# Where half of a causal mask is applied: matmuls on TensorE or selects on GpSimd, in a fused attention and gated-conv kernel

## The chip, the cores and the metric

The kernel runs on one core of a Trainium2 chip. The metric is the device time of one launch in microseconds (us); lower is better. The core has five engines that work side by side, each through its own instructions in order: TensorE (PE, matmuls and transposes; its weight loads are listed as PEld), VectorE (DVE), ScalarE (ACT), GpSimd (POOL) and SyncE (SP, which here only issues DMAs). PE writes its results to PSUM, DVE and ACT read PSUM, and POOL works on SBUF alone.

## The reference

For 8 batches with 8 heads each, 576 positions and 64 numbers per head, an attention with a decay and a causal mask is computed, and behind it a feed-forward layer with a convolution of width 3 along the positions as its gate:

```python
scores = scale * np.matmul(q, k.transpose(0, 1, 3, 2))
log_f = np.log(np.clip(f, 0.0001, 1.0))
cum = np.cumsum(log_f, axis=-1)
decay = cum[:, :, :, None] - cum[:, :, None, :]
causal = np.triu(np.ones((S, S), dtype=bool), k=1)
scores = np.where(causal, -1000000000.0, scores + decay)
attn = np.exp(scores - max)                      # then divided by its row sum
x = (attn @ v)                                   # heads side by side: 576 x 512 per batch
h = np.maximum(x @ w_in, 0.0)                    # 512 -> 1024
conv_out[s] = w0 * h[s - 1] + w1 * h[s] + w2 * h[s + 1]   # per channel
out = (h * sigmoid(conv_out)) @ w_out            # 1024 -> 512
```

All inputs and the output are float32.

## The kernel before

**Tiles and stages.** The unit of the attention is a half batch (hb, 0 to 15): four heads of one batch. Its scores are computed transposed (keys on the 128 partitions, queries along the free axis), in blocks of 128 keys; only blocks on and below the diagonal exist. A pair of heads (i = 2 hb or 2 hb + 1) has its four diagonal blocks per head in one PSUM tile of 128x1024 (`diag_scores`, L344, task sd) and the blocks below the diagonal in one such tile per head (`off_scores`, L366, so). The last 64 keys of all four heads make a tile of 128x256 (`tail_scores`, L324, st). ACT takes the exponential of each (ed L353, eo L371, et L332) into SBUF, `pv` (L384) multiplies with v and a column of ones, in two parts (pv.0, pv.1), DVE divides by the row sum (`norm`, L399, tasks n and m), and the result is transposed by PE (`turn`, t) and copied out by DVE or ACT (tx), or transposed by DMA (tx of hb 11 to 15).

Per batch the feed-forward layer runs over 8 blocks of 128 channels: `ffn1` (L427, task f) on PE, ReLU on ACT (r, L442), the convolution in two instructions on DVE (c L448, d L450), the gate's tanh or sigmoid on ACT (a, L453), the product on DVE (g, L460 or L458), and `ffn2` (L471, task o) on PE over chunks of 128 positions, whose result is evicted from PSUM by ACT or DVE (e, L481; the last batch in parts, L492) and stored by a DMA (s).

**The mask.** On the diagonal blocks half of the scores has to go. There are two ways in the code, chosen per half batch by `MASK_PE` (L88). In it are hb 0 to 7 before the change: PE first writes -1e30 onto the masked places with a matmul of an identity and a constant `mask` (`masked`, L321), one of 128x512 per head of a pair and one of 128x256 for the tail, and the scores are added to that; the exponential goes straight into the f16 tile that pv reads. For the other half batches the scores are not masked; the exponential goes into an f32 tile (`pd`, two buffers, or `p3`, two buffers), and POOL copies it into the f16 tile with an affine_select that writes 0 where the key comes after the query (`diag_mask` L357, task md; `tail_mask` L336, task mt). pv waits for md and mt there, in place of ed and et.

**The decay and the constants.** The decay enters the scores as extra rows of q and k: row images are written to DRAM (ki, L279: three DMAs; zc, L283: four DMAs from tiles that hold 1, -1 and 0) and read back into the q and k tiles (rw, L200: two DMAs, for hb 1 to 7; fi, L193, from hb 8 on). The 1 and -1 (`plus`, `minus`, L253) lie in the second buffer of pd. Half batch 0 adds its decay by matmuls (L317, L319) and doesn't wait for the image. The chain in front of it is dca (DVE, L534), dcl (ACT, L268), dcs (a scan on DVE, L272), dck (DVE, L275 and L276). q and k of hb 0 and 1 are loaded plainly (ld), transposed by PE (tp, L166) and clamped out of PSUM by ACT or DVE (cl, L172, L174); from hb 2 on they come by transposing DMAs (q, L180), clamped in SBUF by DVE (cl, L186) up to hb 7.

**Order.** Nothing is scheduled at run time. Each of these steps is a task with a name, its engine or a choice of engines, its predecessors and the buffers that it takes and gives back (four PSUM tiles, six of pp, two of pd, five of ht, four of u and so on). The string `ORDER` (L17) lists all tasks in one sequence, with the engine behind an @ where there is a choice: the casts of v to f16 (va, L219 and L221) and of the weights (wic, woc, L526) by POOL, ACT or DVE, the copies tx, the evictions e, and the queue that issues ki, rw and the last stores. Each engine executes its tasks in the order of that string, and buffers are handed on in that order too.

Of the kernel before, what the change touches and what calls it, by code (L numbers as in the profile page):

```python
# [56 lines left out]
def kernel(  # L57
# [274 lines left out]
    def tail_exp(hb):  # L332
        o = pt_t[slot[f"et{hb}", "pt"]] if hb in MASK_PE else p3_t[slot[f"et{hb}", "p3"]]
        nc.scalar.activation(o, ps_of(f"st{hb}")[:, 0:HH * SL].rearrange("p (h j) -> p h j", j=SL), AF.Exp, scale=SCALE)
# [18 lines left out]
    def diag_exp(i):  # L353
        o = pair(i)[:, :, 0:512] if i // 2 in MASK_PE else pd_t[slot[f"ed{i}", "pd"]]
        nc.scalar.activation(o, ps_of(f"sd{i}").rearrange("p (s c) -> p s c", s=2), AF.Exp, scale=SCALE)  # L355
# [345 lines left out]
```

## Time and profile before

| | |
|---|---|
| runs of the kernel | 245.07, 245.49, 247.19 us (median 245.49) |
| the profiled execution | its record gives the span from the first to the last instruction, 244.7 us; no time of its own beside it; the median of the runs is 0.8 us above the span |
| granted clock of TensorE | mean 0.993 of full speed |
| instructions | 6393, of which 2627 matmuls |
| DMA | 49.68 MB moved, mean 203 GB/s |

How to read the profile: times are in microseconds from the start of the span, the mean of a group is in nanoseconds. "L322" is line 322 of the kernel. In a group's row stand the line, the engine, the operation, output and inputs by tile name, the shapes and the count; then busy time and mean duration of one; then the idle time of the engine just before these instructions and what ended it. A row of the timeline has start and duration of an instruction (or of several merged ones), and in brackets the idle time in front of it and what released it. A row of busy times by stretch has the stretch, its length, and the busy time of each engine in it with the number of instructions, the granted clock, the share of DMA and its rate. Matmuls are pipelined: a matmul's own duration is longer than the distance to the next one, so PE's pace is read from the distances in the chain of work that ended last. A wait for several semaphores is put down to the one that came last.

### The profile page before, as it was taken

Reading aid. Unit: us, or ns where it says so; the run is one execution under the profiler, and the core shown is the slowest. Engines: PE = TensorE matmul, PEld = TensorE weight load, DVE = VectorE, ACT = ScalarE, POOL = GpSimd, SP = SyncE. Lnnn points to the kernel's source line nnn. Section 1 sums busy time; section 2 is a strip of 40 time slices with the busy share of each in tenths; the row PEclk is TensorE's granted clock in tenths of the full one; section 3 lists DMA queues with packets and bytes.
Section 4 is the critical chain, followed back from the end, with each engine's and each line's share of the span. In section 5 each row is a group of like instructions: output and inputs, shape, how many; then the busy total and the mean of one; then the engine's idle time right before and its main releaser. Section 6 shows DMA issues by size and latency. Waiting matters only on the chain.

```text
span 244.7 us, 6393 instructions
## 1 busy us (share of the span) xinstructions
PE 228.6 (93%) x2627; PEld 146.1 (60%) x2627; DVE 205.5 (84%) x324; ACT 206.8 (85%) x278; POOL 51.9 (21%) x77
## 2 busy tenths in 40 slices
...
GB/s 189 334 169 250 278 184 189 223 198 306 196 216 196 169 182 220 238 268 251 224 212 274 194 198 269 270 102 196 265 198 227 195 209 4 106 173 77 171 85 216
DMA packets 120424, 49.68 MB, mean 203 GB/s; under 512 B 109879, under 2 KB 110647, under 8 KB 120395
## 3 DMA queue, kind: packets, MB, share of 16 engines
...
q10 hardware_dynamic: 322, 0.47, 0.6%
q8 instruction: 20, 0.33, 0.6%
...
HBM read 21.11 MB, written 10.17 MB: 128 GB/s over the span
## 4 chain that ended last, share of the span: by engine, by line
PE 81%; DMA 5%; DVE 5%; ACT 5%; issue 1%; SPq 1%; ACTq 0%; DVEq 0%
PE ps L476 26%; PE ps L431 23%; PE ps L314 15%; PE ps L391 7%; DMA qk<-image 3%; PE ps L322 3%; PE ps L396 3%; DMA u<-in_f_dram 2%; PE ps L416 2%; ACT qk L172 2%; DVE u L450 2%; DVE u L448 1%; ACT ht L442 1%; ACT pp L372 1%; PE ps L317 1%
## 5 line engine op out<-in xcount | busy, mean ns | idle before, releaser
L431 PE MATMUL ps<-xt,w_in_f 128*128 128x512 f16 (+1 forms) x512 | 71.0, 288 | 0.4 <-DVE xt L419 0.4
L372 ACT ACTIVATE pp<-ps 128x1024 f16<-128x1024 f32 x64 | 64.8, 1032 | 3.7 <-PE ps L314 2.3
L476 PE MATMUL ps<-w_out_f,hg 128*128 128x512 f16 x288 | 66.8, 379 | 0.0
L314 PE MATMUL ps<-qk 128*128 128x128 bf16 (+2 forms) x576 | 63.9, 241 | 2.1 <-DMA qk<-image 0.9
L448 DVE SCALAR_TENSOR_TENSOR u<-ht,cwt 128x576 f32<-128x576 f16 x64 | 52.4, 832 | 4.4 <-ACT ht L442 4.2
L450 DVE SCALAR_TENSOR_TENSOR u<-ht,cwt,u 128x576 f32<-128x576 f16 x64 | 53.9, 856 | 0.5
L453 ACT ACTIVATE hg<-u,cw 128x576 f16<-128x576 f32 x64 | 48.7, 782 | 6.1 <-DVE u L450 6.0
L431 PEld LDWEIGHTS <-w_in_f 128*128 128x128 f16 x512 | 34.7, 99 | 29.4 <-issue 1.3
L314 PEld LDWEIGHTS <-qk 128*128 128x128 bf16 x576 | 39.4, 98 | 19.2 <-issue 2.5
L442 ACT ACTIVATE ht<-ps 128x576 f16<-128x576 f32 x64 | 41.0, 664 | 6.4 <-PE ps L431 2.8
L476 PEld LDWEIGHTS <-hg 128*128 128x128 f16 x288 | 26.9, 98 | 28.9
L460 DVE SCALAR_TENSOR_TENSOR hg<-hg,ht 128x576 f16<-128x576 f16 x51 | 38.6, 767 | 0.6 <-ACT hg L453 0.5
L358 POOL TENSOR_SCALAR_AFFINE_SELECT pp<-pd 128x1024 f16<-128x1024 f32 x16 | 19.7, 1244 | 53.6 <-ACT pd L355 53.6
L391 PE MATMUL ps<-va,pp 128*128 128x65 f16 x640 | 25.3, 194 | 1.7 <-DVE va L219 1.7
L391 PEld LDWEIGHTS <-pp 128*128 128x128 f16 x640 | 23.0, 98 | 4.2 <-DVE va L219 1.9
L407 DVE TENSOR_TENSOR xm<-ps,rc 128x896 f16<-128x896 f32 (+1 forms) x32 | 23.9, 751 | 0.5
L355 ACT ACTIVATE pp<-ps 128x1024 f16<-128x1024 f32 x16 | 16.6, 1038 | 5.2 <-PE ps L314 4.0
L219 POOL CAST va<-vf 128x1024 f16<-128x1024 f32 x8 | 10.0, 1247 | 34.3 <-PE ps L314 18.8
L355 ACT ACTIVATE pd<-ps 128x1024 f32<-128x1024 f32 x16 | 16.2, 1023 | 1.2 <-PE ps L314 0.5
L405 DVE RECIPROCAL rc<-ps 128x14 f32<-128x14 f32 (+1 forms) x32 | 6.6, 207 | 10.2 <-PE ps L396 4.9
L322 PE MATMUL ps<-mask,ident 128*128 128x512 bf16 (+1 forms) x40 | 14.4, 364 | 0.4 <-ACT pp L372 0.3
L481 ACT COPY ob<-ps 128x1024 f32<-128x1024 f32 (+1 forms) x14 | 12.9, 918 | 0.3 <-issue 0.2
...
## 6 DMA issues: line engine op xcount, KB each, us to landing
...
```

Of the source, the lines that this page charges most:

```text
L314: nc.tensor.matmul(o, tk[:, h * S + k0:h * S + k0 + 128], tq[:, h * S + q0:h * S + q0 + n], start=first, stop=last and not by_matmul(hb, h))
L355: nc.scalar.activation(o, ps_of(f"sd{i}").rearrange("p (s c) -> p s c", s=2), AF.Exp, scale=SCALE)
L372: nc.scalar.activation(pair(i)[:, s, 512:1536], ps_of(f"so{i}.{s}"), AF.Exp, scale=SCALE)
L391: nc.tensor.matmul(ps[:, c:c + D + 1], block(hb, h, m, n), va[:, h, m, 0:D + 1], start=(m == 0), stop=(m == n))
L407: nc.vector.tensor_tensor(xm[:, CUT * D * u:CUT * D * u + nj * k * D].rearrange("p (j x d) -> p j x d", x=k, d=D), got[:, :, :, 0:D], r.un ...
L431: nc.tensor.matmul(ps[:, t0:t1], w_in_f16[:, cc, 128 * ff:128 * (ff + 1)], xt[:, cc // 2, x:x + t1 - t0], start=(cc == 0), stop=(cc == NCC ...
L442: nc.scalar.activation(ht_of(b, ff)[:, 2:2 + S], ps_of(f"f{b}.{ff}")[:, 0:S], AF.Relu, scale=1.0 if (b, ff) in LATE else 0.5)
L448: nc.vector.scalar_tensor_tensor(u, ht[:, 1:1 + S], cwt[:, ff, 0:1], ht[:, 2:2 + S], op0=ALU.mult, op1=ALU.add)
L450: nc.vector.scalar_tensor_tensor(u, ht[:, 3:3 + S], cwt[:, ff, 1:2], u, op0=ALU.mult, op1=ALU.add)
L453: nc.scalar.activation(hg_of(b, ff), u_t[slot[f"c{b}.{ff}", "u"]], AF.Sigmoid if (b, ff) in LATE else AF.Tanh, scale=cw[:, ff, 1:2])
L460: nc.vector.scalar_tensor_tensor(hv, hv, 1.0, ht_of(b, ff)[:, 2:2 + S], op0=ALU.add, op1=ALU.mult)
L476: nc.tensor.matmul(ps[:, 512 * j:512 * (j + 1)], w, w_out_f16[:, ff, :], start=(ff == 0), stop=(ff == NFF - 1))
```

## The change

`MASK_PE` is cut to half batches 0 to 3. For hb 4 to 7 the mask matmuls go (16 of 128x512 and 4 of 128x256), their exponentials write f32 tiles, and eight tasks md8 to md15 and four tasks mt4 to mt7 are added on POOL. The tile of zeros becomes 128 partitions high, and 1 and -1 are held in its upper half instead of in a buffer of pd. ORDER is replaced as a whole.

```diff
-    MASK_PE = (0, 1, 2, 3, 4, 5, 6, 7,)
+    MASK_PE = (0, 1, 2, 3,)
...
-    zero = cpool.tile([64, 2 * S], BF16, name="zero")
+    zeros = cpool.tile([128, 2 * S], BF16, name="zeros")
+    zero = zeros[0:64]
...
-    signs = pd_t[1].rearrange("p s c -> p (s c)").bitcast(BF16)
-    plus, minus = (signs[0:BH, x * S:(x + 1) * S] for x in range(2))
+    plus, minus = (zeros[BH:128, x * S:(x + 1) * S] for x in range(2))
```

In the new ORDER these tasks have another engine:

| tasks | before | after |
|---|---|---|
| va2.0, va9.0, va15.0, va1.1 | DVE | POOL |
| va3.0, va3.1, va4.0, va5.1, va11.1, va12.1, va14.0, va15.1 | ACT | POOL |
| va8.0, va7.1 | ACT | DVE |
| va8.1; va9.1; va14.1 | DVE; POOL; POOL | ACT; ACT; DVE |
| wic3, woc2 | POOL | DVE |
| e1.1, e2.1, e3.2, e5.1 | ACT | DVE |
| e7.3, e7.1.1; e7.4, e7.1.0 | DVE; ACT | ACT; DVE |
| tx0; tx10 | DVE; ACT | ACT; DVE |
| cl0.0.0, cl1.1.1 | ACT | DVE |
| ki, rw1, rw2; rw5 | SP; ACT | ACT; SP |
| s7.2 | SP | ACT |

Its beginning, up to the first ffn1, in the order of each engine (before, then after):

```
PE   cw tp0.0.0 tp0.0.1 tp0.1.0 tp0.1.1 sd0 so0.1 tp1.0.0 so0.0 tp1.0.1 sd1 tp1.1.0 tp1.1.1 so1.1 so1.0 st0 pv0.0 sd2 so2.1 st1 so2.0 sd3 so3.1 so3.0 pv0.1 sd5 pv1.0 so5.1 t0 pv1.1 sd4 t1 f0.0
PE   tp0.0.0 tp1.0.0 cw tp0.0.1 tp0.1.0 tp0.1.1 tp1.0.1 sd0 tp1.1.0 so0.0 tp1.1.1 so0.1 sd1 so1.0 so1.1 sd2 st1 so2.1 pv0.0 sd3 st0 so3.0 so3.1 sd4 so2.0 pv0.1 sd5 pv1.0 t0 pv1.1 so5.1 t1 so4.1 st2 f0.0
DVE  dca dcs dck cwt cl0.1.1 cl1.0.1 va1.1 cl1.1.0 cl2.0 cl2.1 n0.0 m0.0 n0.1 m0.1 n1.0 m1.0 tx0 n1.1 m1.1 tx1 cl3.0 cl3.1 c0.0
DVE  dca cl0.0.0 dcs cwt dck cl1.0.1 cl0.1.1 cl1.1.0 cl1.1.1 cl2.0 cl2.1 n0.0 m0.0 cl3.0 n0.1 cl3.1 m0.1 n1.0 m1.0 n1.1 m1.1 tx1 wic3 c0.0
ACT  dcl cl0.0.0 cl0.0.1 cl0.1.0 ed0 eo0.1 eo0.0 cl1.0.0 ed1 cl1.1.1 eo1.1 eo1.0 et0 ed2 eo2.1 et1 eo2.0 ed3 eo3.0 eo3.1 ed5 eo5.1 ed4 r0.0
ACT  dcl cl1.0.0 cl0.0.1 cl0.1.0 ki ed0 eo0.0 rw1 eo0.1 ed1 eo1.0 eo1.1 ed2 et1 rw2 eo2.1 ed3 et0 eo3.0 eo3.1 eo2.0 ed4 ed5 tx0 eo5.1 eo4.1 r0.0
SP   ld0.0.0 ld0.1.0 ld0.0.1 v0.0 ld0.1.1 ld1.0.1 ld1.0.0 v0.1 v0.2 v0.3 v0.4 ki q2.1 q2.0 wi1 rw1 wi0 wi2 wi3 rw2 q3.0 q3.1 q4.1 v1.0
SP   ld0.0.0 ld1.0.0 ld0.0.1 ld0.1.1 ld0.1.0 ld1.0.1 v0.0 q2.1 v0.2 v0.1 v0.3 q2.0 v0.4 q3.0 q3.1 wi0 wi1 v1.0 wi3 wi2 rw3 q5.0
```

POOL's list around the new masks, and the end of PE's list:

```
POOL after   va1.0 va0.0 va1.1 va0.1 wic0 wic1 wic2 va2.0 va2.1 va3.0 va3.1 woc0 md9 woc3 woc1 md8 mt4 va4.0 va5.0 va5.1 md11 md10 mt5 md13 md12 va6.0 va6.1 mt6 md14 md15 mt7 md19 md18
PE after     ... sd13 so13.1 pv5.1 sd12 t4 so12.0 t5 so13.0 so12.1 f2.0 f2.1 sd15 so15.0 f2.2 st6 pv6.0 st7 f2.3 ...
PE after     ... o7.4.6 o7.3.5 o7.4.7 o7.1.1 o7.2.4 o7.3.6 o7.2.5 o7.0.5 o7.3.7 o7.1.2 o7.0.6 o7.2.6 o7.1.3 o7.0.7 o7.2.7 o7.1.4 o7.1.5 o7.1.6 o7.1.7
```

More of the change, by code (lines that the diff above doesn't have):

```diff
@@ new lines @@
+ld0 ld1 ld0.0.0 ld1.0.0 tp0.0.0 tp1.0.0 dca cl0.0.0@DVE ld0.0.1 dcl dcs cw ld0.1.1 cwt ld0.1.0 cl1.0.0@ACT dck tp0.0.1
+tp0.1.0 ld1.0.1 tp0.1.1 v0.0 cl0.0.1@ACT tp1.0.1 cl0.1.0@ACT cl1.0.1@DVE ki@ACT q2.1 sd0 cl0.1.1@DVE v0.2 v0.1 tp1.1.0
+ed0 v0.3 q2.0 so0.0 tp1.1.1 cl1.1.0@DVE so0.1 cl1.1.1@DVE va1.0@POOL v0.4 eo0.0 sd1 rw1@ACT q3.0 so1.0 eo0.1 ed1 so1.1
+cl2.0 va0.0@POOL sd2 eo1.0 eo1.1 cl2.1 st1 ed2 et1 so2.1 pv0.0 sd3 rw2@ACT va1.1@POOL q3.1 n0.0 m0.0 st0 va0.1@POOL
+wi0 so3.0 eo2.1 so3.1 ed3 cl3.0 wic0@POOL wi1 et0 wic1@POOL eo3.0 sd4 v1.0 eo3.1 so2.0 pv0.1 wi3 eo2.0 n0.1 cl3.1 sd5
@@ new lines @@
+wi2 pv1.0 m0.1 ed4 n1.0 ed5 m1.0 t0 pv1.1 so5.1 tx0@ACT n1.1 m1.1 rw3@SP eo5.1 q5.0 t1 v1.1 tx1@DVE wic3@DVE so4.1 st2
+eo4.1 v1.3 f0.0 f0.1 r0.0 f0.2 r0.1 so5.0 c0.0 et2 d0.0 r0.2 wic2@POOL v1.4 f0.3 f0.4 c0.1 c0.2 h0 v1.2 a0.0 g0.0 d0.1
+q4.1 eo5.0 r0.3 so4.0 f0.5 r0.4 d0.2 eo4.0 a0.2 sd6 cl5.0 r0.5 c0.4 so6.1 so6.0 c0.5 f0.6 ed6 g0.2 eo6.0 q4.0 sd7
+so7.0 va2.0@POOL d0.5 r0.6 eo6.1 d0.4 va2.1@POOL c0.3 v2.0 a0.1 a0.4 pv2.0 pv2.1 n2.0 m2.0 ed7 st3 n2.1 eo7.0
+va3.0@POOL cl4.1 m2.1 so7.1 cl4.0 d0.3 t2 eo7.1 va3.1@POOL wo0 pv3.0 f0.7 rw4@ACT c0.6 q5.1 wo3 et3 g0.4 v2.4 wo1
@@ new lines @@
+pv3.1 d0.6 n3.0 tx2@ACT n3.1 r0.7 st4 a0.6 m3.0 m3.1 a0.3 sd9 et4 g0.6 ed9 t3 tx3@DVE sd8 c0.7 cl5.1 g0.1 ed8 so9.1
+woc0@POOL g0.3 wo2 eo9.1 rw5@SP md9 d0.7 so8.1 eo8.1 f1.0 r1.0 a0.5 c1.0 f1.1 v2.1 q6.0 a0.7 g0.5 f1.2 r1.2 r1.1 f1.3
+f1.4 so9.0 woc3@POOL f1.5 g0.7 d1.0 r1.3 sd10 woc2@DVE h1 r1.4 v2.2 a1.0 woc1@POOL c1.1 g1.0 d1.1 eo9.0 c1.3 md8 ed10
+a1.1 o0.0 sd11 o0.1 ed11 c1.2 so10.0 c1.4 d1.2 r1.5 so10.1 v2.3 q6.1 d1.3 e0.0@ACT eo10.0 eo10.1 so8.0 f1.6 g1.1 mt4
+eo8.0 r1.6 o0.2 c1.5 d1.4 st5 va4.0@POOL d1.5 pv4.0 so11.1 et5 cl6.0 va5.0@POOL so11.0 va4.1@DVE a1.5 o0.3 cl6.1 g1.5
@@ new lines @@
+a1.4 q7.0 n4.0 eo11.1 va5.1@POOL c1.6 md11 md10 eo11.0 m4.0 pv4.1 f1.7 n4.1 cl7.0 q7.1 a1.3 e0.1@ACT v3.0 r1.7 rw6@SP
+m4.1 pv5.0 sd13 so13.1 cl7.1 n5.0 mt5 v3.2 m5.0 a1.2 q8.1 ed13 pv5.1 n5.1 sd12 t4 m5.1 eo13.1 g1.4 ed12 so12.0 md13 t5
+so13.0 tx4@DVE md12 eo12.0 v3.4 tx5@DVE g1.2 eo13.0 v3.3 so12.1 c1.7 eo12.1 f2.0 r2.0 f2.1 rw7@SP r2.1 g1.3 sd15
+so15.0 v3.1 va6.0@POOL ed15 eo15.0 f2.2 st6 d1.6 c2.0 et6 q9.1 d1.7 d2.0 pv6.0 st7 va6.1@POOL n6.0 c2.1 r2.2 f2.3 et7
+sd14 m6.0 a1.6 a1.7 mt6 ed14 f2.4 zc pv6.1 g1.7 md14 r2.4 h2 d2.1 a2.0 f2.5 n6.1 m6.1 g1.6 so15.1 o1.0 a2.1 r2.3 g2.0
@@ new lines @@
+so14.1 eo15.1 r2.5 q9.0 g2.1 c2.2 q8.0 md15 t6 va7.0@DVE eo14.1 f2.6 d2.2 fi9 q10.0 c2.4 a2.2 r2.6 mt7 tx6@DVE fi8
+c2.6 g2.2 so14.0 o1.1 eo14.0 f2.7 e1.0@ACT r2.7 sd19 pv7.0 st9 v4.0 q11.1 va7.1@DVE sd18 c2.5 v4.3 c2.7 q11.0 ed19
+n7.0 et9 v4.2 d2.4 pv7.1 v4.1 m7.0 ed18 n7.1 o1.2 so19.0 so18.1 md19 s0.0 m7.1 d2.5 a2.4 c2.3 d2.7 q10.1 d2.3 a2.5 t7
+o1.3 eo18.1 g2.5 eo19.0 v4.4 sd17 a2.3 tx7@DVE ed17 e1.1@DVE fi11 f3.0 s1.0 sd16 g2.4 fi10 a2.7 r3.0 g2.3 f3.1 md18
+ed16 r3.1 so18.0 d2.6 c3.1 f3.2 r3.2 eo18.0 a2.6 v5.0 va9.0@POOL so16.1 o1.4 c3.0 so16.0 eo16.1 f3.3 eo16.0 f3.4 d3.0
@@ new lines @@
+g3.7 f4.2 r4.1 f4.3 c4.1 g3.4 eo21.1 r4.2 mt10 r4.0 f4.4 d4.1 c4.0 va10.0@POOL q12.0 s1.2 r4.3 so22.1 d4.0 so23.0
+so21.0 c4.3 md20 h4 r4.4 eo23.0 eo22.1 eo21.0 o3.0 va11.0@POOL st11 c4.4 q13.0 d4.4 d4.3 a4.4 et11 c4.2 so23.1 d4.2
+o3.1 a4.0 pv10.0 va10.1@DVE eo23.1 a4.1 n10.0 pv10.1 e3.0@ACT a4.2 m10.0 g4.1 mt11 n10.1 g4.4 pv11.0 fi12 n11.0 a4.3
+fi13 f4.5 m10.1 r4.5 m11.0 va11.1@POOL f4.6 sd25 g4.0 q15.1 so25.0 r4.6 v6.0 sd24 pv11.1 ed25 n11.1 s3.0 m11.1 ed24
+c4.5 f4.7 eo25.0 md25 r4.7 sd27 d4.5 g4.2 sd26 t10 tx10@DVE ed27 g4.3 o3.2 a4.5 md24 so27.0 md27 o3.3 eo27.0 so24.0
```

24 lines of the change are left out of this document (23 added, 1 removed).

## The prediction, made before the result was known

> **What bounds the kernel now.** I read the page first, then busy time by stretch, then what VectorE (DVE) waits for, then single groups and pieces of the timeline.
>
> ```profile
> span 244.7 us, 6393 instructions
> ...
> PE 228.6 (93%) x2627; PEld 146.1 (60%) x2627; DVE 205.5 (84%) x324; ACT 206.8 (85%) x278; POOL 51.9 (21%) x77
> ...
> PE 81%; DMA 5%; DVE 5%; ACT 5%; issue 1%; SPq 1%; ACTq 0%; DVEq 0%
> ```
>
> TensorE (PE) carries 81% of the chain that ended last. Shares of the whole span hide the stages, so I cut at the first and last conv work of DVE, c0.0 at 39.9 and the end of g7.7 at 236.2. Columns: length, then busy time of PE, weight loads, DVE, ACT, POOL with counts, granted clock, DMA share, GB/s.
>
> ```profile
> 39.90:236.20 196.30, 193.50 (x2196) 119.62 (x2195) 183.19 (x274) 179.72 (x249) 40.04 (x39) 0.99 0.90 197
> ```
> ```profile
> 62.00:110.00 48.00, 47.99 (x583) 30.89 (x583) 46.13 (x70) 46.02 (x65) 4.66 (x5) 1.00 1.04 210
> ```
> ```profile
> 50.40:53.90 3.50, 3.50 (x36) 2.27 (x33) 3.12 (x6) 3.50 (x6) 0.00 (x0) 0.51 1.18 250
> ```
>
> In those 196.3 us PE is idle for 2.8, DVE for 13.1 and ACT for 16.6. PE sets the pace, but two engines stand close behind it: from 62 to 110, where the masks to be removed lie, PE has no idle time and DVE 1.9 us in 48. The third row is a stretch at half the granted clock. In front of it lies the longest idle time of PE behind the start-up:
>
> ```profile
> 49.99 1.62 PE L391 MATMUL ps<-va,pp 128*128 128x65 f16 x32 [1.67 <-DVE va L219]
> ```
> ```profile
> 151.56 1.73 PE ps L476 x8
> ```
>
> pv2.0 waits 1.67 us for va2.0, which stands on DVE behind conv work; then 3.5 us at 0.51 lose another 1.7. The second row is the chain: eight 128x512 matmuls in 1.73, so 0.216 us for 512 columns. That is PE's real pace; the durations of 380 ns in the groups overlap.
>
> **The change part by part.** The groups that price it (mean ns of one after the comma):
>
> ```profile
> L358 POOL TENSOR_SCALAR_AFFINE_SELECT pp<-pd 128x1024 f16<-128x1024 f32 x16 | 19.7, 1244 | 53.6 <-ACT pd L355 53.6
> ...
> L322 PE MATMUL ps<-mask,ident 128*128 128x512 bf16 x32 | 12.4, 386 | 0.4 <-ACT pp L372 0.3
> ...
> L219 POOL CAST va<-vf 128x1024 f16<-128x1024 f32 x8 | 10.0, 1247 | 34.3 <-PE ps L314 18.8 <-DMA vf<-in_v_dram 10.0 <-PE ps L431 5.5
> ...
> L526 POOL CAST w_out_f<-ob 128x1024 f16<-128x1024 f32 x4 | 5.5, 1392 | 13.4 <-DMA ob<-in_moe_w_out_dram 13.4
> ...
> L481 DVE COPY ob<-ps 128x1024 f32<-128x1024 f32 x3 | 3.7, 1219 | 2.0 <-ACT xt L419 1.9
> L219 DVE CAST va<-vf 128x1024 f16<-128x1024 f32 x4 | 3.6, 910 | 0.5 <-DMA out_dram<-ob 0.5
> ...
> L337 POOL TENSOR_SCALAR_AFFINE_SELECT pt<-sel_q 128x256 f16<-128x256 f32 x4 | 2.6, 644 | 23.0 <-ACT sel_q L334 23.0
> ...
> L322 PE MATMUL ps<-mask,ident 128*128 128x256 bf16 x8 | 2.1, 272 | 0.0
> ...
> L492 DVE COPY u<-ps 128x512 f32<-128x512 f32 x2 | 1.4, 692 | 2.1 <-ACT ob L492 1.9 <-PE ps L476 0.2
> ```
>
> *Masks off PE.* Half batches 4 to 7 lose half of the 32 and half of the 8: 16 x 0.216 + 4 x 0.108 = 3.9 us. The exponentials keep their length (their output turns from f16 to f32). POOL gains eight selects at 1.244 and four at 0.644: 12.5 us.
>
> *The stall.* va2.0 moves to POOL, behind casts that end early. So 1.67 + 1.7 = 3.4 us more can go from PE. If something else is late there (sd7 or so7.0 hold their PSUM slots longer), nothing is gained: 0 to 3.4. PE alone could then end at 244.7 - 3.9 - 3.4 = 237.4.
>
> *Work that changes engines.* After c0.0, DVE gains the evictions e1.1, e2.1, e5.1 (3 x 1.22), e3.2 (0.69), the cast woc2 (taken as a cast of va, 0.91), tx10 (0.75, the rows below), and goes from four large casts of va to two (-1.82) and from three small ones to four (below half of a large one; 0.3): 4.5 us. ACT loses those evictions, tx10, four large casts and four small ones net: at DVE's prices 3.7 + 0.7 + 0.8 + 3.6 + 1.2, some 10 us. POOL gets six large casts of va (7.5) and three small ones (1.5), gives woc2 (-1.4): with the masks 20 us on top of 40.
>
> *POOL against DVE.* Where the two meet, the trace shows an instruction of DVE that takes 0.81 or 0.82 by itself doubled:
>
> ```profile
> 39.85 0.81 DVE L448 SCALAR_TENSOR_TENSOR u<-ht,cwt 128x576 f32<-128x576 f16 x1
> ```
> ```profile
> 120.36 0.82 DVE L450 SCALAR_TENSOR_TENSOR u<-ht,cwt,u 128x576 f32<-128x576 f16 x1
> 121.09 0.75 DVE L460 SCALAR_TENSOR_TENSOR hg<-hg,ht 128x576 f16<-128x576 f16 x1
> 121.76 1.65 DVE L450 SCALAR_TENSOR_TENSOR u<-ht,cwt,u 128x576 f32<-128x576 f16 x1
> 123.34 1.58 DVE L219 CAST va<-vf 128x1024 f16<-128x1024 f32 x1
> ```
> ```profile
> 121.39 2.98 POOL L358 TENSOR_SCALAR_AFFINE_SELECT pp<-pd 128x1024 f16<-128x1024 f32 x2 [7.39 <-ACT pd L355]
> ```
> ```profile
> L450 DVE SCALAR_TENSOR_TENSOR u<-ht,cwt,u 128x576 f32<-128x576 f16 x64 | 53.9, 856 | 0.5
> L448 DVE SCALAR_TENSOR_TENSOR u<-ht,cwt 128x576 f32<-128x576 f16 x64 | 52.4, 832 | 4.4 <-ACT ht L442 4.2
> ...
> L460 DVE SCALAR_TENSOR_TENSOR hg<-hg,ht 128x576 f16<-128x576 f16 x51 | 38.6, 767 | 0.6 <-ACT hg L453 0.5
> ```
>
> Two selects in a row cost DVE 0.83 and, against the mean cast of 0.91, 0.67: 1.5 us in 2.98. On average it is far less: the means of the three conv groups lie 41 and 17 ns above 815 and 17 above 750, so 64 x 0.041 + 64 x 0.017 + 51 x 0.017 = 4.6 us, with that slow cast 5.3 us in 40 us of POOL, 0.135 for each. For 20 us more I take 2.7; the ends are 0 (all in DVE's idle time) and 0.5 x 20 = 10.
>
> The Trainium skill speaks against this part: "SBUF — State Buffer", section "Who interferes with whom", has a DVE instruction with two SBUF inputs and a GpSimd instruction that reads SBUF fight for one port, which the first holds to its end while the other stands still. By that rule alone, with DVE always the later, the 20 us would cost DVE nearly 20, with POOL always the later nothing; the average of this trace is near the second, the pair at 121 us near the first.
>
> *New waits.* pv4 to pv7 now wait for POOL instead of ACT. In POOL's queue md12 stands in front of va6.0, and pv6.0 needs both: that is the closest place.
>
> ```profile
> 89.15 1.02 ACT L355 ACTIVATE pp<-ps 128x1024 f16<-128x1024 f32 x1 [0.21 <-PE ps L314]
> ```
> ```profile
> 94.81 0.99 PE ps L391 x32
> ```
>
> That exponential (ed12) ends at 90.2; one select and one cast end at 92.7, at the pace of the slow pair above at 93.2; pv6.0 begins at 94.8. So cover is 1.5 us or more; without it PE idles for the difference, and past some 1.7 the half clock comes back.
>
> *Constants.* plus and minus move into a tile of their own partitions: same memsets, same DMAs. It lets ed8 and ed9 write pd before zc has sent the rows. Nothing.
>
> *Start-up.* On DVE cl0.0.0 goes ahead of the scan, and the weight ratios ahead of dck; q of half batch 1 is loaded second.
>
> ```profile
> 8.37 1.36 DVE L272 TENSOR_TENSOR_SCAN u<-one,u 128x576 f32<-128x576 f32 x1 [0.75 <-ACT u L268]
> ...
> 10.26 0.76 DVE L276 SCALAR_TENSOR_TENSOR kc<-u,kc 64x576 bf16<-64x576 f32 x1
> ...
> 12.22 0.58 PE L322 MATMUL ps<-mask,ident 128*128 128x512 bf16 x1
> ...
> 12.29 1.47 DVE L174 TENSOR_SCALAR qk<-ps,lim 128x1152 uint16<-128x1152 uint16 x1
> ```
>
> The copy of 1.47 fills the 0.75 us in which the scan waited and 0.7 more, and the ratios, which filled the time from dck's end at 11.0 to 12.3, come ahead of it: dck ends at 11.0 + 0.7 + 1.3 = 13.0. sd0, at 12.2 before, starts 0.8 late; PE uses the time for two more transposes of inputs (0.5 each) that came later before. Net 0. ki's three DMA issues and rw1's and rw2's two each move from SP to ACT, past SP's weight and q loads; behind ki only ed0 stands, which waits for sd0; behind rw1 (which waits for the last clamp, cl1.1.1) stands eo0.1, perhaps 1 us. ACT loses two clamps for it; rw5 goes back to SP and s7.2 to ACT, an issue or two each, beside other work. I take 0, bounds -1 and +2. At the end of it tx0 goes to ACT:
>
> ```profile
> 35.75 0.75 DVE L419 COPY xt<-ps 128x1152 f16<-128x1152 f16 x1
> ...
> 37.51 0.76 DVE L419 COPY xt<-ps 128x1152 f16<-128x1152 f16 x1 [0.46 <-PE ps L416]
> ```
>
> The second copy released f0.0; it can come 0.65 sooner, so c0.0 starts at 39.2.
>
> **The sum.** PE alone would end at 237.4, but DVE can't follow: its 183.2 become 183.2 + 4.5 + 2.7 = 190.4 us. What stays of its 13.1 us of idle time is the term that decides. Its waits from 62 to 228 us:
>
> ```profile
> DVE u L448 <- ACT ht L442: 3.3, 8, 0.6
> DVE ob L481 <- ACT xt L419: 1.9, 1, 1.9
> DVE xt L419 <- PE ps L416: 1.4, 4, 0.6
> DVE rc L405 <- PE ps L396: 0.8, 3, 0.4
> DVE rc L405 <- PE ps L391: 0.8, 2, 0.6
> DVE hg L460 <- ACT hg L453: 0.5, 2, 0.3
> ```
>
> 5.7 us were for ACT, which gets 10 us lighter, and 3.0 for PE, which gets 7 lighter. I take both away: 13.1 - 8.7 = 4.4; the ends are 0 and 13.1. Behind the end of g7.7 lay 8.5 us, 21 matmuls of 0.216 in it; the new list has 17 from the first that needs g7.7: 7.6. So 39.2 + 190.4 + 4.4 + 7.6 = 241.6 us of span. The median of the runs shown, 245.49, stands 0.8 above the profiled span: 242.4.
>
> **The rivals.**
>
> *PE keeps setting the pace.* DVE's idle time goes to nearly 0 and the POOL meetings fall into it: 237.4 + 0.8 = 238.2, or 241.7 if the stall is only replaced. For it: the chain is 81% PE, and ACT's relief unties DVE. Against it: it needs DVE busy for 98 to 100% of 190 us, and no stretch above has more than 96%.
>
> *The start-up or a late POOL result takes the gain back.* A stall like that at 48 us in a new place, with half clock, costs 3.4; from 242.4 that gives 245.8, no change. For it: an order that is new throughout; against it: the 1.5 us of cover at pv6.0.
>
> *DVE becomes the bound and POOL holds it (slower).* If each us of added POOL work costs DVE 0.5 instead of 0.135, as at 121 us, that is 10 instead of 2.7: 242.4 + 7.3 = 249.7. It turns into a loss from 2.7 + 3.1 = 5.8 us, 0.29 for each. For it: the masks land where DVE has 4% of air. This is the rule of "SBUF — State Buffer" with DVE the later one half of the time.
>
> **How the numbers follow.** The forecast 242.4 has 0.45 (its own range 240.3 to 244.5), PE keeps the pace 0.25, no change by a new stall 0.13, slower by the port 0.17. The range 238.0 to 248.5 leaves out the lower edge of the second and the worse half of the last. 1% is 2.45 us, about what a measurement here can tell from nothing: faster is below 243.0. That is 0.6 of the forecast and nearly all of PE's case: 0.27 + 0.23 = 0.50; slower 0.17; same 0.33.
>
> **What would show it.** Right: 20 mask matmuls at L322; no wait for va ahead of pv2.0 and no half clock near 50 us; between c0.0 and g7.7 DVE busy for about 190 us with under 6 idle, and PE with several us of idle time, released by DVE or ACT. The terms: means of the three conv groups of DVE (856, 832 and 767 now) up by 10 to 20 ns; the time of c0.0 (39.2). Wrong: DVE idle by over 8 us while PE stands still too (a wait that I don't see), selects that release pv6.0, or a PE that is busy throughout while the span goes below 239.

## The result, and the profile after

The change made the kernel slower: 264.81 us (median; 263.24 to 266.15) against 245.56 us, ratio 1.078 with an interval of 1.0712 to 1.0847. The forecast was 242.4 with a range up to 248.5; the kernel went the other way. Of the variants below, e4, e5 and e10 had executions that took longer than the rest of theirs (up to 599.57 us in e5); their medians and ratios leave these out, and e4's profile is of one of them (257.2 us). In the profile after, the lines of the untouched code stand 52 or 53 further down (L448 is now L500, L358 is L410, L219 is L272). The head of the page:

```profile
span 262.0 us, 6376 instructions
...
PE 229.7 (88%) x2607; PEld 145.8 (56%) x2607; DVE 233.0 (89%) x330; ACT 197.5 (75%) x264; POOL 82.0 (31%) x97
...
DVE 46%; PE 42%; ACT 4%; issue 4%; DMA 2%; ACTq 0%; SPq 0%; DVEq 0%
```

What sets the pace has changed: DVE carries 46% of the chain that ended last, where it carried 5%, and PE 42% instead of 81%. DVE is busy for 27.5 us more than before, though only a few pieces of work were moved onto it. Busy time by stretch, from the first conv instruction (c0.0) to the end of the last gate (g7.7), and for the stretch in which the removed masks lay:

```profile
37.90:252.80 214.90, 193.46 (x2170) 118.61 (x2169) 208.37 (x278) 171.20 (x235) 70.83 (x60) 0.98 0.83 183
...
62.00:115.00 53.00, 46.49 (x574) 29.82 (x573) 52.72 (x70) 43.62 (x60) 21.60 (x19) 0.97 0.88 172
```

DVE is busy for 208.4 of 214.9 us, and for all but 0.3 of the 53 us of the second row. PE, which had 2.8 us of idle time between these two points, now has 21.4. The groups show where DVE's time comes from:

```profile
L500 DVE SCALAR_TENSOR_TENSOR u<-ht,cwt 128x576 f32<-128x576 f16 x64 | 59.7, 948 | 1.6 <-ACT ht L494 1.5
L502 DVE SCALAR_TENSOR_TENSOR u<-ht,cwt,u 128x576 f32<-128x576 f16 x64 | 58.8, 936 | 0.5
...
L410 POOL TENSOR_SCALAR_AFFINE_SELECT pp<-pd 128x1024 f16<-128x1024 f32 x24 | 34.2, 1434 | 59.9 <-ACT pd L407 59.9
...
L512 DVE SCALAR_TENSOR_TENSOR hg<-hg,ht 128x576 f16<-128x576 f16 x51 | 47.3, 945 | 0.6 <-ACT hg L505 0.6
...
L272 POOL CAST va<-vf 128x1024 f16<-128x1024 f32 x14 | 17.8, 1280 | 50.8 <-DMA vf<-in_v_dram 50.8
```

There are as many instructions in the three conv groups as before (64, 64 and 51), and each does the same work; but their means went from 832, 856 and 767 to 948, 936 and 945 ns. By the prediction's own formula, 64 x (mean - 815), again 64 x (mean - 815), and 51 x (mean - 750), that is 8.5 + 7.7 + 9.9 = 26.2 us of lengthening, where the trace of before had 4.6. The selects grew too, from a mean of 1244 to 1434 ns. How that comes about is seen best where one engine runs conv work while the other has several tasks in a row. DVE, then POOL, of the same stretch:

```profile
187.73 0.75 DVE L512 SCALAR_TENSOR_TENSOR hg<-hg,ht 128x576 f16<-128x576 f16 x1
188.39 1.59 DVE L500 SCALAR_TENSOR_TENSOR u<-ht,cwt 128x576 f32<-128x576 f16 x1
189.91 1.64 DVE L502 SCALAR_TENSOR_TENSOR u<-ht,cwt,u 128x576 f32<-128x576 f16 x1
191.47 1.58 DVE L512 SCALAR_TENSOR_TENSOR hg<-hg,ht 128x576 f16<-128x576 f16 x1
192.98 0.81 DVE L502 SCALAR_TENSOR_TENSOR u<-ht,cwt,u 128x576 f32<-128x576 f16 x1
```
```profile
188.28 1.09 POOL L272 CAST va<-vf 128x1024 f16<-128x1024 f32 x1 [9.73 <-DMA vf<-in_v_dram]
189.33 1.61 POOL L410 TENSOR_SCALAR_AFFINE_SELECT pp<-pd 128x1024 f16<-128x1024 f32 x1
190.89 1.55 POOL L272 CAST va<-vf 128x1024 f16<-128x1024 f32 x1
```

POOL runs a cast, a select and a cast back to back; exactly three instructions of DVE take 1.6 us instead of 0.75 to 0.82, and the next one, with POOL idle, takes 0.81 again. From the second POOL task on, both engines are slow: they take turns.

The waits moved with it. PE's longest idle time behind the start-up is no longer at pv2.0 but at 69 us. One row each of PE's and ACT's timeline, and busy time by stretch:

```profile
69.20 1.01 PE L366 MATMUL ps<-qk 128*128 128x64 bf16 x4 [3.06 <-ACT ht L494]
```
```profile
67.83 0.78 ACT L505 ACTIVATE hg<-u,cw 128x576 f16<-128x576 f32 x1 [3.33 <-DVE u L502]
```
```profile
66.00:68.00 2.00, 0.14 (x2) 0.04 (x1) 2.00 (x3) 0.17 (x1) 1.20 (x2) 1.00 1.10 230
68.00:70.00 2.00, 0.80 (x4) 0.45 (x4) 2.00 (x4) 2.00 (x4) 0.00 (x0) 0.60 1.03 232
70.00:72.00 2.00, 2.00 (x13) 0.89 (x10) 2.00 (x4) 2.00 (x4) 0.00 (x0) 0.54 1.53 239
```

Read backwards: PE waits 3.06 us for a PSUM tile that ACT's ReLU (L494) has to empty; ACT was itself idle for 3.33 us, waiting for DVE's `u`; DVE is busy without a gap (2.00 of 2.00 in each row). When PE goes on, its clock is near half of full speed. So the delay is paid twice on PE, as idle time and in a slower clock.

### The profile page after: what moved, and what is told of

Read it like the earlier page. It is cut to its first block, busy times and chain, and to the rows that moved or that the text cites. A ratio compares the mean times of both kernels' runs of the same rounds, so it can differ in the third digit from the quotient of the medians.

```text
span 262.0 us, 6376 instructions
## 1 busy us (share of the span) xinstructions
PE 229.7 (88%) x2607; PEld 145.8 (56%) x2607; DVE 233.0 (89%) x330; ACT 197.5 (75%) x264; POOL 82.0 (31%) x97
## 4 chain that ended last, share of the span: by engine, by line
DVE 46%; PE 42%; ACT 4%; issue 4%; DMA 2%; ACTq 0%; SPq 0%; DVEq 0%
DVE u L500 13%; PE ps L528 13%; DVE hg L512 12%; DVE u L502 10%; PE ps L483 10%; PE ps L366 7%; PE ps L443 4%; DVE qk L239 3%; DVE xm L459 3%; PE ps L219 2%; DMA hg<-in_q_dram 2%; PE ps L448 2%; DVE xt L471 2%; DVE ob L533 2%; ACT hg L505 1%
## 5 line engine op out<-in xcount | busy, mean ns | idle before, releaser
L424 ACT ACTIVATE pp<-ps 128x1024 f16<-128x1024 f32 x64 | 63.5, 1023 | 6.4 <-PE ps L371 3.5
L500 DVE SCALAR_TENSOR_TENSOR u<-ht,cwt 128x576 f32<-128x576 f16 x64 | 59.7, 948 | 1.6 <-ACT ht L494 1.5
L502 DVE SCALAR_TENSOR_TENSOR u<-ht,cwt,u 128x576 f32<-128x576 f16 x64 | 58.8, 936 | 0.5
L410 POOL TENSOR_SCALAR_AFFINE_SELECT pp<-pd 128x1024 f16<-128x1024 f32 x24 | 34.2, 1434 | 59.9 <-ACT pd L407 59.9
L494 ACT ACTIVATE ht<-ps 128x576 f16<-128x576 f32 x64 | 40.6, 653 | 14.1 <-DVE hg L512 5.8
L512 DVE SCALAR_TENSOR_TENSOR hg<-hg,ht 128x576 f16<-128x576 f16 x51 | 47.3, 945 | 0.6 <-ACT hg L505 0.6
L272 POOL CAST va<-vf 128x1024 f16<-128x1024 f32 x14 | 17.8, 1280 | 50.8 <-DMA vf<-in_v_dram 50.8
L407 ACT ACTIVATE pd<-ps 128x1024 f32<-128x1024 f32 x24 | 24.3, 1026 | 2.3 <-PE ps L366 1.9
L239 DVE TENSOR_SCALAR qk<-qk,lim 128x2304 uint16<-128x2304 uint16 x12 | 11.0, 924 | 3.4 <-DMA qk<-in_q_dram 3.4
L219 PE MATMUL ps<-ident_b,hg 128*128 128x128 bf16 x72 | 7.6, 289 | 6.0 <-DMA hg<-in_q_dram 6.0
L219 PEld LDWEIGHTS <-hg 128*128 128x128 bf16 x72 | 6.6, 134 | 6.2 <-DMA hg<-in_q_dram 6.2
```

The source lines that it names most:

```text
L410: nc.gpsimd.affine_select(pair(i)[:, :, 0:512].rearrange("p s (m j) -> p s m j", j=128), pd_t[slot[f"ed{i}", "pd"]].rearrange("p s (m j) - ...
L424: nc.scalar.activation(pair(i)[:, s, 512:1536], ps_of(f"so{i}.{s}"), AF.Exp, scale=SCALE)
L494: nc.scalar.activation(ht_of(b, ff)[:, 2:2 + S], ps_of(f"f{b}.{ff}")[:, 0:S], AF.Relu, scale=1.0 if (b, ff) in LATE else 0.5)
L500: nc.vector.scalar_tensor_tensor(u, ht[:, 1:1 + S], cwt[:, ff, 0:1], ht[:, 2:2 + S], op0=ALU.mult, op1=ALU.add)
L502: nc.vector.scalar_tensor_tensor(u, ht[:, 3:3 + S], cwt[:, ff, 1:2], u, op0=ALU.mult, op1=ALU.add)
L512: nc.vector.scalar_tensor_tensor(hv, hv, 1.0, ht_of(b, ff)[:, 2:2 + S], op0=ALU.add, op1=ALU.mult)
```

## The experiments

My theory: every POOL instruction that reads SBUF and meets a conv instruction of DVE lengthens it by some 0.7 us; the sum of these meetings, on an engine with 3% of idle time, is the loss. The first rival: the new order is bad by itself (stalls, half clock, POOL results that come late), and the longer instructions are a side effect. The second: the added masks alone cost it. Medians, ratios to the kernel before on the same chip (with intervals), and the lengthening by the formula above:

| kernel | us | ratio | lengthening, us |
|---|---|---|---|
| before | 245.56 | 1 | 4.6 |
| after | 264.81 | 1.078 (1.0712 to 1.0847) | 26.2 |
| e1_write_only_masks | 250.53 | 1.0205 (1.0185 to 1.0226) | 10.5 |
| e2_write_only_pool | 243.85 | 0.9935 (0.9913 to 0.9957) | 0.7 |
| e3_new_order_pe_masks | 259.17 | 1.054 (1.0485 to 1.0595) | 18.8 |
| e6_new_order_old_casts | 261.91 | 1.0624 (1.0566 to 1.0683) | 20.6 |
| e7_new_order_alone | 256.13 | 1.0428 (1.0384 to 1.0472) | 15.1 |
| e12_new_order_write_only | 248.05 | 1.0094 (1.0058 to 1.0131) | 0.8 |
| e4_old_order_pool_masks | 252.92 | 1.0318 (1.0273 to 1.0363) | see there |
| e5_old_order_new_casts | 251.1, 248.9 | 1.0167 (1.0097 to 1.0237) | 10.4 |
| e11_one_half_batch | 247.13 | 1.0046 (1.0013 to 1.0079) | 6.9 |
| e10_va2_on_pool | 247.14 | 1.0025 (0.9981 to 1.0069) | 6.1 |
| e9_before_write_only | 246.46 | 1.0018 (0.9985 to 1.005) | 0.6 |

**The same kernel with POOL only writing.** e1 leaves ORDER and every task where it is, but its masks fill their tile without reading, and the exponential writes the f16 tile in place of the f32 one; e2 does the same to POOL's casts of v, which then no longer wait for v to be loaded either.

```diff
 def diag_exp(i):
-    o = pair(i)[:, :, 0:512] if i // 2 in MASK_PE else pd_t[slot[f"ed{i}", "pd"]]
+    o = pair(i)[:, :, 0:512]
 def diag_mask(i):
-    nc.gpsimd.affine_select(pair(i)[:, :, 0:512]..., pd_t[slot[f"ed{i}", "pd"]]..., ...)
+    nc.gpsimd.memset(pair(i)[:, :, 0:512], 0.5)
...
+    if e == "POOL":                                   # e2 only
+        nc.gpsimd.memset(va[:, :, 0:4, 0:D] if part == 0 else va[0:SL, :, 4, 0:D], 0.5)
```

> The changed kernel (264.8 us), but all 36 masks of GpSimd write a constant instead of reading scores: the exponential goes straight into the f16 tile and a memset of the same tile follows it, so that the order, the engine and the wait of pv for GpSimd stay (left out: the mask and the diagonal scores). Theory 'shared reading' (a GpSimd instruction that reads SBUF holds up VectorE instructions with two SBUF inputs): the selects stand beside about 15 us of lengthened VectorE instructions in the changed trace, so about 250 us (247 to 254), and the means of the three conv groups fall from 948, 936, 945 to about 880. Rival 'the order' (the new list makes engines wait whatever GpSimd does): 262 to 266. Rival 'late masks' (pv waits for GpSimd): 262 to 266, since the chain is as long.

> As e1, and the casts of v on GpSimd are memsets too (left out as well: half of v). Shared reading: nearly all lengthening goes, 238 to 244 us, conv means at 820 to 840. The order: 258 or more. Late masks: as e1, 260 or more, since masks still come from GpSimd.

Measured: 250.53 and 243.85 us. The groups of e1, then of e2, and e2's busy time from c0.0 to the end of g7.7:

```profile
L495 DVE SCALAR_TENSOR_TENSOR u<-ht,cwt 128x576 f32<-128x576 f16 x64 | 55.3, 878 | 2.8 <-ACT ht L489 2.6
...
L408 POOL MEMSET pp<- 128x1024 f16 x24 | 22.6, 951 | 59.6 <-ACT pp L405 59.6
```
```profile
L497 DVE SCALAR_TENSOR_TENSOR u<-ht,cwt 128x576 f32<-128x576 f16 x64 | 50.8, 808 | 3.3 <-ACT ht L491 2.9
L499 DVE SCALAR_TENSOR_TENSOR u<-ht,cwt,u 128x576 f32<-128x576 f16 x64 | 51.5, 822 | 0.5
...
L410 POOL MEMSET pp<- 128x1024 f16 x24 | 22.7, 952 | 77.0 <-ACT pp L407 77.0
L509 DVE SCALAR_TENSOR_TENSOR hg<-hg,ht 128x576 f16<-128x576 f16 x51 | 38.1, 764 | 0.5 <-ACT hg L502 0.4
```
```profile
39.56:233.06 193.50, 187.84 (x2170) 116.37 (x2169) 182.87 (x278) 170.58 (x235) 44.39 (x60) 1.00 0.93 202
```

POOL still runs 60 tasks in the stretch, at the same places of every queue and each for about 0.95 us where it was a mask of 128x1024. It lengthens nothing: 808, 822 and 764 ns. DVE's busy time is 182.9 instead of 208.4 us with the same 278 instructions, and the whole loss is gone: 264.81 to 243.85, of which 14.3 us go with the masks' reading and 6.7 with the casts'. This rules out the first rival in its plain form. Stalls and half clock went too (in that stretch PE is idle for 5.7 us instead of 21.4, at a granted clock of 1.00), so in the kernel after they follow from a late DVE.

**The order, the masks and the casts apart.** e3 takes the new ORDER without the twelve added mask tasks, with the masks of hb 4 to 7 back on PE. e6 is the kernel after with the 17 casts of v that changed engine back on their old ones. e7 does both, so that the new order alone is left, with POOL's selects and casts of v those of before.

```diff
-MASK_PE = (0, 1, 2, 3,)                                    # e3, e7; their ORDER lacks md8 to md15 and mt4 to mt7
+MASK_PE = (0, 1, 2, 3, 4, 5, 6, 7,)
-va1.1@POOL va2.0@POOL va3.0@POOL va3.1@POOL va4.0@POOL va5.1@POOL va7.1@DVE ...    # e6, e7
+va1.1@DVE va2.0@DVE va3.0@ACT va3.1@ACT va4.0@ACT va5.1@ACT va7.1@ACT ...
```

> The new list without md8 to md15 and mt4 to mt7, masks of half batches 4 to 7 by matmuls again. Shared reading: these 12 stand beside some 8 us of lengthening in VectorE, which is the bound; 3.9 us of matmuls come back on TensorE, which waits anyway: 256 to 260. The order: 264.8 plus up to 3.9, 265 to 269. Late masks: 262 to 266, the waits of TensorE between 80 and 115 us go and the matmuls come.

> The changed kernel with those 17 casts back on the engines of before; masks of half batches 4 to 7 stay on GpSimd. Shared reading: casts stand beside 10 us of lengthening in the changed trace, so 250 to 256. The order: 262 to 267.

> The new list with neither: masks on TensorE and the 17 casts on their old engines. What is left is the new sequence, the evictions on VectorE and the start. Shared reading: near before, 243 to 250. The order: 256 or more.

Measured: 259.17, 261.91 and 256.13 us. Two of my numbers fell: e6 should have come to 250 to 256 and e7 to 243 to 250. I had reckoned the loss by how much POOL works; but e7, with POOL's selects and casts of v as in the kernel before, has 15.1 us of lengthening instead of 4.6. Of the 19.2 us of loss, the new order alone makes 10.6 (245.56 to 256.13), the masks then 5.8 (to 261.91), the casts then 2.9; taken the other way round, by e3, the casts make 3.0 and the masks 5.6. The added masks alone, the second rival, are less than a third. So either the order is bad for another reason, as the rival says, or the same POOL work meets DVE differently in it. e12 tells these apart: e7 with the masks and casts of v that are left on POOL only writing, as in e2.

> e7 (new list, masks on TensorE, casts of v on their old engines; 256.1 us) with the masks and casts that GpSimd still has as memsets. Shared reading (e7 is slow because the new list puts the same GpSimd work beside conv work, where the old one puts it beside work from PSUM): 243 to 248. The order (its own waits): 253 to 257.

Measured: 248.05 us, just above the first of these two ranges. One row each of the groups of e7 and of e12, then the busy time between c0.0 and g7.7 of e7 and of e12:

```profile
L511 DVE SCALAR_TENSOR_TENSOR hg<-hg,ht 128x576 f16<-128x576 f16 x51 | 44.8, 895 | 0.1
```
```profile
L508 DVE SCALAR_TENSOR_TENSOR hg<-hg,ht 128x576 f16<-128x576 f16 x51 | 38.9, 781 | 0.9 <-ACT hg L501 0.8
```
```profile
39.34:245.20 205.86, 194.39 (x2190) 119.19 (x2189) 197.18 (x279) 176.57 (x243) 45.87 (x39) 1.00 0.86 190
```
```profile
37.14:236.86 199.72, 193.18 (x2190) 118.90 (x2189) 183.65 (x279) 176.67 (x243) 30.24 (x39) 1.00 0.93 197
```

With the same order and 279 instructions, DVE loses 13.5 us of busy time, and 8.1 of the 10.6 us are gone. The order costs some 2.5 us by itself, and 8 through its meetings.

Where POOL's tasks fall is the difference. In the kernel before, a pair of selects stands in POOL's and DVE's timeline like this:

```profile
109.89 2.15 POOL L358 TENSOR_SCALAR_AFFINE_SELECT pp<-pd 128x1024 f16<-128x1024 f32 x2 [19.24 <-ACT pd L355]
```
```profile
109.65 1.09 DVE L407 TENSOR_TENSOR xm<-ps,rc 128x896 f16<-128x896 f32 x1
110.66 0.17 DVE L405 RECIPROCAL rc<-ps 128x4 f32<-128x4 f32 x1
110.86 0.42 DVE L407 TENSOR_TENSOR xm<-ps,rc 128x256 f16<-128x256 f32 x1
111.56 0.76 DVE L419 COPY xt<-ps 128x1152 f16<-128x1152 f16 x1 [0.28 <-PE ps L416]
```

Both engines run at full pace: 1.08 us for each select, 1.09 for the normalisation, 0.76 for the copy. DVE reads PSUM there (`xm<-ps`, `rc<-ps`, `xt<-ps`). Going through the timelines, I count by what DVE was doing when a POOL task began between c0.0 and g7.7: one of the three conv groups in 21 of 39 cases before, in 29 of 38 in e7 and in 50 of 60 after. Of the tasks on 128x1024 alone, which cost most, it is 11 of 26, 18 of 25 and 32 of 40. Why the new order puts them there isn't settled; that it does is what the counts show.

**The price of a meeting, by itself.** e8 is the kernel before with stretches appended in which DVE repeats one instruction, alone, beside six selects, or beside six fills. It was executed once.

```diff
+for vec, n, pool, m in ((conv_like, 10, None, 0), (conv_like, 14, select, 6), (conv_like, 14, fill_only, 6),
+                        (gate_like, 14, select, 6), (norm_like, 8, None, 0), (norm_like, 10, select, 6),
+                        (evac_like, 8, select, 6), (clamp_like, 10, select, 6)):
```

> The kernel of before with eight short stretches behind its last task, on tiles that are free by then (its time is longer by those and is not used; read the rows). conv_like is L448 again, gate_like L460 on 512 columns, norm_like L407 (one input in PSUM), evac_like L481 (input in PSUM only), clamp_like L186. Shared reading: beside six selects in a row, conv_like and gate_like take 0.7 to 0.9 us longer about once per select, and selects grow from 1.1 to 1.6; beside six memsets nothing grows; norm_like and evac_like stay as they are beside selects, and selects stay at 1.1; clamp_like is held up like conv_like. A general slowing by any GpSimd work: memsets slow conv_like too, and norm_like suffers as well.

DVE's timeline of the appended part, then POOL's:

```profile
242.19 6.80 DVE L684 SCALAR_TENSOR_TENSOR u<-ht,cwt 128x576 f32<-128x576 f16 x8
...
249.03 16.20 DVE L684 SCALAR_TENSOR_TENSOR u<-ht,cwt 128x576 f32<-128x576 f16 x14
...
265.26 11.92 DVE L684 SCALAR_TENSOR_TENSOR u<-ht,cwt 128x576 f32<-128x576 f16 x14
...
277.84 14.05 DVE L687 SCALAR_TENSOR_TENSOR pp<-ht 128x512 f16<-128x512 f16 x13
...
292.94 7.84 DVE L690 TENSOR_TENSOR xm<-ps,rc 128x896 f16<-128x896 f32 x7
...
300.81 11.22 DVE L690 TENSOR_TENSOR xm<-ps,rc 128x896 f16<-128x896 f32 x10
...
321.93 0.88 DVE L699 TENSOR_SCALAR qk<-qk,lim 128x2304 uint16<-128x2304 uint16 x1
...
322.84 12.11 DVE L699 TENSOR_SCALAR qk<-qk,lim 128x2304 uint16<-128x2304 uint16 x9
```
```profile
249.18 9.46 POOL L676 TENSOR_SCALAR_AFFINE_SELECT pp<-pd 128x1024 f16<-128x1024 f32 x6 [44.38 <-DVE pp L705]
265.37 5.99 POOL L681 MEMSET pp<- 128x1024 f16 x6 [6.74 <-DVE pp L705]
277.28 8.97 POOL L676 TENSOR_SCALAR_AFFINE_SELECT pp<-pd 128x1024 f16<-128x1024 f32 x6 [5.92 <-DVE pp L705]
300.94 6.93 POOL L676 TENSOR_SCALAR_AFFINE_SELECT pp<-pd 128x1024 f16<-128x1024 f32 x6 [14.68 <-DVE pp L705]
```

Alone, the conv instruction takes 6.80 / 8 = 0.85 us. Fourteen of them take 11.9 us beside six fills, as alone, and 16.2 beside six selects: 4.3 us more, 0.71 for each select. The selects pay as well: 9.46 / 6 = 1.58 us each, against 1.16 beside DVE work that reads PSUM, where DVE pays nothing either (1.12 us alone and beside them). The gate on 512 columns is held up like the conv instruction: thirteen take 14.05 us where one ahead of them took 0.69, 0.85 more for each select. The eviction from PSUM is not (seven in 8.77 us, 1.25 each, against 1.22 for the one ahead of them). The clamp of q (one SBUF tile in and out, 16-bit; 0.88 us for the one just ahead of the nine) is held up as well: 12.1 us for nine.

**The same parts on the old order.** e4 adds the masks of hb 4 to 7 on POOL to the old order, each right behind its exponential; e11 does it for hb 7 alone; e5 changes only the engines of the 17 casts of v; e10 moves va2.0 alone; e9 lets the kernel before only write in its masks and casts of v.

```diff
-... sd9 t3 so9.1 st4 ed9 a0.3 et4 eo9.1 sd8 ...           # e4; e11 only md14, md15, mt7
+... sd9 t3 so9.1 st4 ed9 md9 a0.3 et4 mt4 eo9.1 sd8 ...
-... va2.0@DVE ...                                          # e10, and 16 more in e5
+... va2.0@POOL ...
```

> The list of before with the masks of half batches 4 to 7 on GpSimd, each right behind its exponential; nothing else moved. Shared reading: up to 12 x 0.8 us of lengthening where VectorE has 1.9 us of air, against 3.9 us less on TensorE: 247 to 252. The order: 241 to 243, the matmuls go and nothing else is new. Late masks: 246 to 250 with TensorE waiting in front of pv4 to pv7.

> A small dose: the list of before with only half batch 7 masked on GpSimd (two selects of 128x1024 and one of 128x256 more, 1.0 us of matmuls less). Shared reading: e4 lost 8.4 us with 12 selects, so a quarter, 1 to 3 us: 246 to 248.5. The order: 244.5.

> The list of before, masks on TensorE as before, only the 17 casts of v on the engines that the new list gives them (ten more on GpSimd than before). Shared reading: about as much GpSimd work as e4 adds (8 to 10 us instead of 12.5, and VectorE gives two large casts away): 247 to 254. The order: 243 to 246, since ACT and VectorE lose work and the list is the old one.

> The kernel of before with one cast moved: va2.0 from VectorE to GpSimd, the stall of 1.7 us and the half clock behind it that the prediction counted at 3.4 us. If those set the end: 242 to 243. Shared reading: TensorE gains them, but the cast meets conv work at 45 to 48 us, where VectorE has no air: 243.5 to 246. Might be the best version that gives the reference.

> The kernel of before with its 24 masks and 14 casts of v on GpSimd as memsets (left out: those masks with their scores, and those parts of v). Shared reading: the conv means fall from 832, 856, 767 to 820 and 755 at most; TensorE sets the pace there, so only part of the 5 us shows: 241 to 245. The order: 245 to 246. With e2 (243.9) it compares both lists without any reading by masks and casts.

Measured: e4 252.92, e11 247.13, e10 247.14 and e9 246.46 us, and e5 251.1 and 248.9. e4 is above its 247 to 252, and e10 and e9 are above their ranges too. None of the versions that do the whole computation was faster than the kernel before: on the old order the masks on POOL cost 7.4 us, and for one half batch 1.6 (ratio 1.0046, just clear of 1). The casts alone cost some 4.4, from two executions. e4 is no clean measure of the meetings: in its profile a cast of the weights came late behind my inserted tasks in POOL's queue, and that profile's lengthening isn't set beside the others. PE's waits there:

```profile
PE ps L528 <- POOL w_out_f L578: 3.6, 1, 3.6
```

e10 tests a part that the prediction counted on, the stall at pv2.0. PE's waits in e10:

```profile
PE ps L373 <- ACT pp L406: 1.4, 1, 1.4
...
PE ps L442 <- POOL va L270: 0.5, 1, 0.5
```

The wait for va2.0 went from 1.67 to 0.5 us, but a wait of 1.4 for a PSUM tile took its place some 4 us later, with a half clock behind it. Nothing was gained: the interval of the ratio, 0.9981 to 1.0069, includes 1.

e9 was a miss that taught something. I had expected 241 to 245. The groups of e9 show that the lengthening is gone (821, 820 and 748 ns), and the time isn't lower. Its chain, one group, and the busy time from c0.0 to the end of g7.7:

```profile
PE 83%; DVE 7%; DMA 5%; ACT 2%; issue 1%; ACTq 0%; DVEq 0%
...
L445 DVE SCALAR_TENSOR_TENSOR u<-ht,cwt 128x576 f32<-128x576 f16 x64 | 51.6, 821 | 5.2 <-ACT ht L439 4.9
```
```profile
39.67:236.73 197.06, 193.61 (x2198) 119.92 (x2195) 179.75 (x274) 180.23 (x249) 28.78 (x38) 0.99 0.91 197
```

DVE is idle there for 17.3 us instead of 13.1. So before the change PE sets the pace, and the 4.6 us of meetings lie in DVE's idle time. After it little is left to cover them: DVE's idle time is 6.5 us.

## Why the prediction was wrong

Its sum by terms, beside what the profile after showed and what e2 showed, in which the meetings are taken out (us):

| term | predicted | after | e2 |
|---|---|---|---|
| start of c0.0 | 39.2 | 37.9 | 39.6 |
| DVE busy to the end of g7.7 | 190.4 | 208.4 | 182.9 |
| DVE idle in it | 4.4 | 6.5 | 10.6 |
| behind g7.7 | 7.6 | 9.2 | 9.0 |
| span | 241.6 | 262.0 | 242.1 |

**The step that failed** is "For 20 us more I take 2.7; the ends are 0 (all in DVE's idle time) and 0.5 x 20 = 10." The lengthening rose by 21.6 us, from 4.6 to 26.2, eight times the value taken and twice the upper end. Of the 20.4 us by which the span exceeds the sum, DVE's busy time makes 18.0. The mechanism was named, with its rows and its loss threshold; the size was taken from the wrong number. 0.135 us per POOL us was an average over where POOL's tasks happened to lie in the order of before, and the change made the order anew: e7, with the selects and casts of v of before, has three times the lengthening. What moves to another order is the price of one meeting (0.83 and 0.67 in the rows at 121 us, 0.71 in e8); the chance of one has to be worked out anew. From rows that stood in the prediction, the three conv groups fill 144.9 of the 196.3 us of that stretch, a chance of 0.74 if POOL's tasks fall where they may. After the change POOL has 24 selects and some 12 large casts of v in the stretch: 36 x 0.74 x 0.71 = 19, and four casts of weights and the small tasks come on top. This estimate would have said slower. It was made after the fact, though, and it isn't a law. For e7, with 25 large tasks, the same rule gives 13.1 us where 15.1 were measured; but for the kernel before, with 26, it gives 13.7 where 4.6 were measured, since only 11 of the 26 began during conv work there. So the chance belongs to the order as well.

**The upper end** failed for the same reason: 0.5 per POOL us was the price of the slow pair, and it was applied to the 20 added us only. But the 40 us that were there could be placed worse too, and were.

**The rule that spoke against it held.** The Trainium skill, "SBUF — State Buffer", section "Who interferes with whom", has a DVE instruction with two SBUF inputs contend with a GpSimd instruction that reads SBUF and not with one that only writes, and a DVE instruction with at most one SBUF input outside its two-port modes not contend at all. e2 and e8 agree on each point: fills cost nothing (11.92 us for 14), selects beside the normalisation from PSUM nothing (1.12 us each), selects beside conv work 0.71 us each. The clamp, whose operation (tensor_scalar) the same section lists among those that can enter a two-port mode, was held up in e8, which fits. The prediction gave this rule's price with DVE always the later, nearly 20 us, as an extreme; 21.6 was measured. (The pair at 121 us, which it put near that extreme, cost 1.5 us in 2.98, so half of it.) One part of the rule is softer here: it lets the second instruction stand still until the first is done, but one select and one conv instruction together took 1.58 us, less than 1.16 + 0.85 = 2.01.

**What held.** The copy and the scan at the start, and, less closely, c0.0 (39.2 predicted; 37.9 after, 39.6 in e2). DVE's work apart from the meetings: 183.2 - 4.6 + 4.5 = 183.1, and e2 has 182.9. PE's busy time: 193.5 - 3.9 - 1.7 = 187.9, and e2 has 187.8, so both the masks off PE and the half clock were sized rightly for a kernel without meetings. With them the stall isn't gone but moved: its wait of 3.06 us at 69 us is again followed by a half clock, the case "if something else is late there", and e10 shows the same in small.

**What else was off.** DVE's idle time is 10.6 in e2, not 4.4: ACT and PE had more waits left than I took away. The tail was 9.2, not 7.6. The step from span to time was 1.7 in the profiled execution after (263.74 and 262.0), not 0.8, since I had compared one execution's span with the median of others. Together these took most of the gain: with no meeting of the masks and casts of v left, the change is worth 0.65% (e2, 0.9935), where the forecast had 1.3% with 2.7 us of meetings still in it. By its own terms without any meeting the span would have been 39.2 + 183.1 + 4.4 + 7.6 = 234.3 us; e2 has 242.1. So even apart from the meetings the sum was 7.8 us short, 6.2 of them in DVE's idle time. The threshold for the half clock, "past some 1.7", wasn't borne out either: in the kernel after PE waited 1.88 us ahead of 49.5 us and 2.13 ahead of 222.5, and the granted clock stayed at 1.00.

**The rivals.** The third had the right mechanism ("DVE becomes the bound and POOL holds it") and the right sign, at a fifth of the loss: 249.7 is 4.2 us, and 19.2 were measured; its condition, 0.29 us for each added POOL us, was passed at 21.6 / 20 = 1.1 (0.7 by POOL's measured busy time, which rose by 30.8 us, from 40.04 to 70.83). The first, PE sets the pace, fell: PE has 21.4 us of idle time. Of the second, a stall in a new place with half clock did come (at 69 us), but DVE's late `u` made it; a late POOL result held PE for 3.6 us in e4's profile and for at most 0.5 us in the others.
